# Chunked attention and a cosine feed-forward layer: turning the probabilities of tiles 2 to 8 with tall VectorE transposes and DMAs between partitions

## The chip, the core and the metric

The kernel runs on one core of a Trainium2 chip. The core has five engines, each with its own instruction queue that runs in program order: TensorE (PE; its weight loads are shown as PEld), VectorE (DVE), ScalarE (ACT), GpSimd (POOL) and SyncE (SP, which here issues all DMAs). The metric is the device time of one execution in microseconds (us); a kernel's time is the median of several runs. Matmuls read SBUF and write PSUM; everything is float32, and a matmul of full precision is made of three products of high and low parts.

## The reference

Attention inside chunks of 64 positions, then a feed-forward layer with g = h cos(h):

```python
# q, k, v: (8 batches, 8 heads, 576 positions, 64), chunks of 64
scores = scale * matmul(q_c, k_c.T)               # 64 x 64 for each batch, head and chunk
attn = exp(scores - max(scores)); attn = attn / (sum(attn) + 1e-9)
out = matmul(attn, v_c)
x = out.transpose(0, 2, 1, 3).reshape(4608, 512)  # 4608 tokens, 8 heads x 64
h = x @ w_in                                      # 512 -> 2048
g = h * cos(h)
result = g @ w_out                                # 2048 -> 512
```

## The kernel before

The 4608 tokens are nine tiles of 512 (t = 0 to 8). A tile has eight chunks, and the eight heads are four pairs (hp = 0 to 3, two heads h each); g is a pair of pairs (hps 2g and 2g+1).

**Attention of a tile.** `scores` makes the 64x64 products of queries and keys in two PSUM banks, VectorE and ScalarE make the probabilities e from them (maximum, difference, exponential, sum, `quotient`). A tile e of 128 partitions holds for each pair two rows of chunks: partition is (parity of the half, query), the free axis (chunk or head, key). For the product with the values the probabilities must be turned: the key goes on the partition. `weighted` (L757) then multiplies each turned 64x64 block (moving operand) with the values (stationary operand), 32 float32 matmuls that show up as 64 matmul instructions, and ScalarE takes the result out into e (L781 or L1609).

**How the probabilities are turned** differs by tile:
- tiles 0 and 1: `transposed` (L725), TensorE transposes of 128x128 against an identity (L731); these stay as they are.
- tile 2: `turned` (L740), for each pair eight VectorE instructions that transpose the 32x32 blocks of 32 partitions x 256 elements and put them where they belong.
- tiles 5 and 7: `turned_together` (L1576), the same for two pairs at once: eight instructions of 32 partitions x 512 for each g.
- tiles 3, 4, 6 and 8: `turned_by_pe` (L1582), four TensorE transposes for each pair (L1585) into a PSUM bank, and a copy by ScalarE or VectorE into the tile pts. Here the scores are laid out by head (`by_head`), the products are made by `weighted_turned` (L1589), and the values must come in another order: `load_values_turned` (L1508) loads them in four DMAs of 64 KB for each pair, in pieces of 512 bytes. The other tiles load them with one DMA of 256 KB (`load_v`).

**The feed-forward layer.** Tiles 0 and 1 are computed plainly (`hidden`, `activated`, `project`); tile 2 and then the pairs of tiles (3, 4), (5, 6) and (7, 8) by a Strassen-like scheme of seven products, for which VectorE, ScalarE and GpSimd make sums and differences and split them in high and low parts (`forms` for x, `split` in `outer` for g). The weights' sums lie in DRAM and are streamed in blocks of 512 KB through six rooms (`load_block`); a block is asked for when the matmuls of the block six before it are done.

**The order of the work.** No engine decides at run time: the program emits one order for each engine. For the first part (tiles 0 and 1, attention of tile 2) it comes from `placed` and `in_order`, with the priorities in the list DUE; for the rest from `planned` (L299) with offsets in MOVED. Both go through estimated durations and lags. In `planned` the main matmuls form one chain; the small matmuls of attention (`main=False`) are put on TensorE at the first seam at which their inputs are estimated to be there, plus CARE = 0.8 us. All DMAs stand in one queue on SP: one that waits for a semaphore holds all that stand behind it.

**Rooms.** `attention_of` (L1981) takes a pair of tiles (ta, tb): it begins both, loads values, and ends both (`attention_ends`, L1613). For tiles 3 and 4 (`alone`) pts has its own two buffers; for tiles 5 to 8 the two pairs of a g share one room of w_in.

Of the kernel before, what the change touches and what calls it, by code (L numbers as in the profile page):

```python
# [11 lines left out]
F32 = mybir.dt.float32  # L12
# [9 lines left out]
P = 128  # L22
TOK = 512
# [78 lines left out]

AHEAD = 4.0
# [27 lines left out]
    158.12, 58.9, 68.58, 63.65, 252.88, 143.8, 82.3, -250.55, 219.35, 114.51, -120.22, -295.86, 1e+09, -4.71,  # L131
# [5 lines left out]
    262.3, 48.25, 126.32, 193.62, 1e+09, 345.43, 23.97, -61.67, 75.14, -1.8, 433.58, 246.37, -62.79, 87.68, -8.61,  # L137
    -145.35, 32, 6.23, 84.32, 191.91, -66.13, 267.53, -107.91, 1e+09, 59.88, 1e+09, 1.78, 1e+09, 6.61, 1e+09,
    1e+09, -10.09, -254.05, 202.29, -15.1, 262.24, -166.36, 249.63, 71.08, 209.64, -226.64, 255.17, -18.33,
# [5 lines left out]
    -76.27, 1e+09, 292.24, -11.78, -101.18, 119.54, 173.07, 246.81, -59.42, 152.58, 59.6, 147.63, -111.18,  # L145
    -165.31, 170.18, 412.05, -234.16, 253.81, 56.94, 223.55, 174.74, 172.68, 262.87, 1e+09, -113.14, 133.26,
# [8 lines left out]
    199.71, 243.39, -154.74, 16.19, 1e+09, 1e+09, 143.88, -50.34, 1e+09, 1e+09, 1e+09, 1e+09, 1e+09, 1e+09,  # L155
    172.37, 92.61, 1e+09, 1e+09, 1e+09, 1e+09, 1e+09, 1e+09, 1e+09, 58.67, 248.55, 155.33, -25.97, 231.79, 141.91,
    1e+09, 1e+09, 153.74, 117.79, 119.81, 83.59, 470.08, 488.44, 258.14, 542.25, -17.83, 164.19, 314.55, 83.71,
    62.74, 350.71, -36.4, 242.13, -61.82, 228.28, 332.92, 1e+09, 437.5, 104.97, 27.99, 78.88, 1e+09, 458.39,
    -62.42, 304.54, 227.74, 1e+09, 424.55, 137.98, 50.14, 154.55, 190.64, 238.98, 240.92, 295.04, 313.65, -63.39,
    266.72, 327.78, 178.57, 212.45, 346.38, 151.22, 291.83, -2.81, 148.05, 154.34,  # L160
# [276 lines left out]
def attention_then_cos_ffn(ctx: ExitStack, tc, qT, kT, v, w_in, w_out, out, wide):  # L437
# [207 lines left out]
    def scores(t, g, banks, by_head=False, by_chunk=False):  # L645
# [3 lines left out]
        for j in range(2):  # L649
            qt, kt = queries.pop((t, 2 * g + j))  # L650
            for c in range(NCH):
# [10 lines left out]
        order_of = "(h r)" if by_head else "(r h)"  # L662
        e = weights_of(t, g).rearrange(f"p a {order_of} k -> p a r h k", h=2)
# [60 lines left out]
    def transposed(t, hp):  # L724
# [1734 lines left out]
```

## Time and profile before

| | |
|---|---|
| median of 3 runs | 806.09 us (805.15 to 806.11) |
| span of the profiled execution, first to last instruction | 804.7 us |
| TensorE busy, matmuls | 791.9 us (98%) |
| TensorE busy, weight loads | 700.4 us (87%) |
| VectorE busy | 692.5 us (86%) |
| ScalarE busy | 530.4 us (66%) |
| GpSimd busy | 203.7 us (25%) |
| DMA | 189.88 MB, 236 GB/s on average |

Busy times are averages over stages with different limits; matmuls are pipelined, and their ends are modelled. Which engine sets the time is read from the stretches and from the chain of work that ended last: it goes back from the last instruction, at each step to what released it.

### The profile page before, as it was taken

The numbers are of one execution on the slowest core, as the hardware profiler recorded it, in microseconds if no ns is written. First come the engines' busy times: TensorE is split into PE (matmuls) and PEld (weight loads), VectorE is DVE, ScalarE is ACT, GpSimd is POOL, SyncE is SP. The second block draws the span as 40 slices with busy tenths as digits, with TensorE's granted clock in tenths as the row PEclk, the third lists the DMA queues.
The fourth block names the chain that finished last, engine by engine and source line by source line (L and its number), as shares of the span: only waits on it lengthen the run. The fifth ranks groups of instructions, "written<-read, shape, count | busy, mean of one in ns | idle before, by whom it ended". The sixth has DMA issues, their size and how long they took to land.

```text
span 804.7 us, 17487 instructions
## 1 busy us (share of the span) xinstructions
PE 791.9 (98%) x6720; PEld 700.4 (87%) x6720; DVE 692.5 (86%) x1071; ACT 530.4 (66%) x1006; POOL 203.7 (25%) x179
## 2 busy tenths in 40 slices
PE   5999999999999999999999999999999999999998
PEld 5888788888988888888999998888999988889998
DVE  6899998888888798999999988899999878789854
ACT  4998856455567756767777566889655566665552
POOL 2373765866812211410410001121001001000000
PEclk9999999999999999999999999999999999999999
DMA  9993748585898896987557779655665665556653
GB/s 319 405 416 117 244 150 295 202 292 198 280 315 249 297 296 222 293 286 260 189 169 257 221 238 323 205 195 192 225 213 195 190 222 191 183 183 210 210 184 105
DMA packets 95266, 189.88 MB, mean 236 GB/s; under 512 B 8656, under 2 KB 51664, under 8 KB 95184
## 3 DMA queue, kind: packets, MB, share of 16 engines
q1 hardware_dynamic: 95184, 188.78, 69.0%
q8 instruction: 53, 0.87, 0.4%
q14 instruction: 29, 0.24, 0.1%
HBM read 148.90 MB, written 39.85 MB: 235 GB/s over the span
## 4 chain that ended last, share of the span: by engine, by line
PE 89%; DMA 4%; DVE 4%; ACT 2%; issue 1%; SPq 0%; DVEq 0%
PE acc L471 55%; PE h L471 29%; PE a L471 5%; DMA w_in<-in_w_in_dram 2%; DMA kt<-in_kT_dram 1%; DVE w L536 1%; PE a L1585 1%; DMA qt<-in_qT_dram 1%; DVE g L832 0%; ACT w L541 0%; ACT g L833 0%; DVE w_in L481 0%; ACT half L543 0%; DVE w_out L475 0%; DVE w_out L481 0%
## 5 line engine op out<-in xcount | busy, mean ns | idle before, releaser
L471 PE MATMUL h<-x,w_in 128*128 128x512 f32 (+1 forms) x852 | 190.6, 367 | 0.0
L471 PEld LDWEIGHTS h<-x,w_in 128*128 128x128 f32 x852 | 148.0, 188 | 27.7 <-DVE g L834 0.3
L471 PE MATMUL acc<-w_in,w_in 128*128 128x512 f32 (+1 forms) x702 | 153.0, 346 | 0.0
L471 PEld LDWEIGHTS acc<-w_in,w_in 128*128 128x128 f32 x702 | 113.5, 188 | 16.5
L471 PE MATMUL acc<-w_out,g_hi 128*128 128x512 f32 x352 | 110.0, 394 | 0.4 <-DVE vt L475 0.4
L471 PE MATMUL acc<-w_in,g_hi 128*128 128x256 f32 x576 | 104.2, 282 | 0.0
L471 PEld LDWEIGHTS acc<-w_in,g_hi 128*128 128x128 f32 x576 | 88.4, 188 | 0.9
L471 PE MATMUL acc<-x,w_in 128*128 128x512 f32 x276 | 82.6, 391 | 0.0
L471 PE MATMUL acc<-w_in,g_lo 128*128 128x256 f32 x288 | 80.3, 279 | 0.0
L471 PEld LDWEIGHTS acc<-w_out,g_hi 128*128 128x128 f32 x352 | 64.2, 188 | 13.3 <-DVE vt L475 0.8
L471 PE MATMUL acc<-w_out,g_lo 128*128 128x512 f32 x176 | 68.7, 391 | 0.0
L1483 ACT ACTIVATE w_out<-w_out 128x512 f32<-128x512 f32 x96 | 60.1, 631 | 11.5 <-DVE w_out L1479 11.2
L481 DVE TENSOR_TENSOR g_lo<-w_out,g_hi 128x512 fp32r<-128x512 f32 x79 | 57.2, 729 | 10.8 <-ACT g_hi L477 9.1
L477 ACT CAST g_hi<-w_out 128x512 fp32r<-128x512 f32 x75 | 46.4, 620 | 28.2 <-PE acc L471 15.6
L471 PEld LDWEIGHTS acc<-x,w_in 128*128 128x128 f32 x276 | 51.5, 188 | 11.1
L471 PEld LDWEIGHTS acc<-w_in,g_lo 128*128 128x128 f32 x288 | 54.3, 189 | 0.0
L481 POOL TENSOR_TENSOR w_out<-g,w_out 128x512 f32<-128x512 f32 x10 | 14.2, 1423 | 143.1 <-ACT w_out L1483 143.1
L477 ACT CAST g_hi<-g 128x512 fp32r<-128x512 f32 x50 | 30.8, 623 | 25.1 <-DVE g L834 12.4
L481 POOL TENSOR_TENSOR g_lo<-w_out,g_hi 128x512 fp32r<-128x512 f32 x8 | 11.7, 1466 | 127.7 <-ACT g_hi L477 53.9
L471 PE MATMUL h<-w_in,g_hi 128*128 128x256 f32 x240 | 43.5, 282 | 0.0
L471 PEld LDWEIGHTS acc<-w_out,g_lo 128*128 128x128 f32 x176 | 33.0, 188 | 7.1
L1476 ACT ACTIVATE w_out<-g 128x512 int32<-128x512 f32 x48 | 29.9, 630 | 13.6 <-DVE g L1492 12.2
(216 smaller groups left out, 1690.9 us busy)
## 6 DMA issues: line engine op xcount, KB each, us to landing
w_in<-combo SPq DMA_DIRECT2D x112, 512.0 KB, 4.3
w_in<-sums SPq DMA_DIRECT2D x84, 512.0 KB, 3.8
combo<-w_in SPq DMA_DIRECT2D x56, 256.0 KB, 3.9
sums<-w_out SPq DMA_DIRECT2D x56, 256.0 KB, 4.4
qt<-in_qT_dram SPq DMA_DIRECT2D x36, 256.0 KB, 5.2
kt<-in_kT_dram SPq DMA_DIRECT2D x36, 256.0 KB, 5.4
w_in<-in_w_in_dram SPq DMA_DIRECT2D x16, 512.0 KB, 9.1
w_out<-in_w_out_dram SPq DMA_DIRECT2D x16, 512.0 KB, 9.9
```

The lines of the kernel that those rows point to most:

```text
L471: kept(nc.tensor.matmul(*args, **kw))
L477: kept(nc.scalar.copy(out=out, in_=in_))
L481: kept(eng.tensor_tensor(out, a, b, op=op))
L536: kept(nc.vector.scalar_tensor_tensor(bits, bits, 3, low, op0=ALU.logical_shift_left, op1=ALU.bitwise_or))
L1476: kept(nc.scalar.activation(n.bitcast(I32), h, AF.Identity, bias=0.25, scale=0.5 / math.pi))
L1483: kept(nc.scalar.activation(g, g, AF.Sin, bias=0.5 * math.pi))
L1585: kept(nc.tensor.transpose(out=pt[:, i * P : (i + 1) * P], in_=e[:, 2 * i : 2 * i + 2].rearrange("p c k -> p (c k)"), identity=ident,))
```

## The change

All tiles from 2 to 8 get the same way of turning, and the code of the others goes. For each unit (one pair of heads in tiles 2, 3 and 4; two pairs in tiles 5 to 8) there are now four steps:
1. one VectorE instruction over all 128 partitions (512 or 1024 elements each) transposes all 32x32 blocks in place of their partitions and sorts them in two areas of pts, by the half of the keys;
2. ScalarE (or VectorE) copies the second area to a spare part of e, which is dead by then;
3. `over`: two DMAs move 32 partitions each of the first area to the second area of 32 other partitions (pieces of 1 KB, or 2 KB for two pairs);
4. `back`: two DMAs move what stood in the second area, from the spare copy, to the first area.

Half of the blocks thereby change partitions, the other half stand right from the start. The turned block of a chunk and head is now two runs of 32 columns, and `weighted` takes it so. The TensorE transposes at L1585, their copies out of PSUM, `by_head`, `weighted_turned` and `load_values_turned` are gone; the values of all these tiles come in one DMA for each pair. The lists DUE and MOVED have new numbers throughout.

```diff
+CROSS = 3.0
...
-    def turned(t, hp):
-
-        pts = att.tile([P, TOK], F32, name="pts")
-        probs[t, hp] = pts
...
-        def piece(par, qb, kb):
-            i, o = (par * CH + x * BL for x in (qb, kb))
-            kept(nc.vector.transpose(out=dst[o : o + BL, :, qb], in_=src[i : i + BL, :, kb]))
...
+    def turned(t, hps, pts):
+
+        g, first = divmod(hps[0], 2)
+        n = len(hps)
+        e = weights_of(t, g)[:, first : first + n]
+        areas = pts.rearrange("p (x n) -> p x n", x=2)
+        spare = e.rearrange("p a c k -> p (a c k)")[:, : n * TOK // 2]
+        for j, hp in enumerate(hps):
+            probs[t, hp] = pts.rearrange("p (x a c q) -> p a c x q", x=2, a=n, q=BL)[:, j]
+
+        def turn_blocks():
+            kept(nc.vector.transpose(
+                out=pts.rearrange("p (x m q) -> p m x q", x=2, q=BL),
+                in_=e.rearrange("p a c (x k) -> p (a c) x k", k=BL),
+            ))
+
+        def put_by(by):
+            copy_by(by, spare, areas[:, 1])
+
+        def crossed(par, x):
+            i = par * CH + x * BL
+            return slice(i, i + BL)
+
+        def over():
+            for par in range(2):
+                load(areas[crossed(par, 0), 1], areas[crossed(par, 1), 0])
+
+        def back():
+            for par in range(2):
+                load(areas[crossed(par, 1), 0], spare[crossed(par, 0)])
+
+        return turn_blocks, put_by, over, back
...
+                        q = pts[ks, fs] if t < FAST else pts[ks, 2 * pr + h]
                         matmul(
-                            banks[par][hs, o : o + CH], vt[ks, fs], pts[ks, fs],
+                            banks[par][hs, o : o + CH], vt[ks, fs], q,
...
                 def go(key=key, hp=hp):
-                    made[key] = turned(t, hp)
+                    made[key] = turned(t, (hp,), att.tile([P, TOK], F32, name="pts"))
                     made[key][0]()
-                pts.append(piece(DVE, 0.44, go, q[hp], w, *partial_out))
-                for i in range(1, 8):
-                    pts.append(piece(DVE, 0.44, rest_of(key, i), pts[-1]))
+                a = piece(DVE, 0.72, go, q[hp], w, *partial_out)
+                a = piece(ACT, 0.36, rest_of(key, 1), a, other=(DVE, 0.3, True))
+                a = piece(SP, 0.15, rest_of(key, 2), a, lag=CROSS)
+                pts.append(piece(SP, 0.15, rest_of(key, 3), a, lag=CROSS))
...
-    def load_values_turned(t, hp):
...
-        for s in range(2):
-            for c in range(2):
-                load(to[s * CH : (s + 1) * CH, :, c], src[c * CH : (c + 1) * CH, :, s])
-        values[t, hp] = vt
...
-            run = (lambda hp=hp: load_values_turned(t, hp)) if by_pe else (lambda hp=hp: load_v(t, hp))
-            v_rooms[t, hp].load = task(SP, 0.4 if by_pe else 0.1, run, new=(v_rooms[t, hp],), lag=5.0)
+            v_rooms[t, hp].load = task(SP, 0.1, lambda hp=hp: load_v(t, hp), new=(v_rooms[t, hp],), lag=5.0)
...
-    def turned_by_pe(t, hp, pt):
...
-        for i in range(NPR):
-            kept(nc.tensor.transpose(
-                out=pt[:, i * P : (i + 1) * P], in_=e[:, 2 * i : 2 * i + 2].rearrange("p c k -> p (c k)"), identity=ident,
...
-    def weighted_turned(t, g, banks):
...
-    def attention_ends(t, quotients, by_pe, alone=False):
+    def attention_ends(t, quotients, alone=False):
...
-            if by_pe:
...
-                for par in range(2):
-                    for qb in range(2):
-                        for kb in range(2):
...
-                                turned_together(t, g, pair_of_pts[t, g], qb, kb, par)
-                            done.append(task(
-                                DVE, 0.75, go, *(done[-1:] or [quotients[hp] for hp in hps]), uses=(e,) if first else (e, *pts_rooms),
...
+            for some in ((hps[:1], hps[1:]) if alone else (hps,)):
+                r = room_of("pts", 2) if alone else room_of(f"w_in{G_ROOM}")
+                rooms.append(r)
+                key = ("t", t, some)
+
+                def begin(some=some, key=key):
+                    if alone:
+                        pts = att.tile([P, TOK], F32, name="pts")
+                    else:
+                        pts = w_in_room(G_ROOM, F32)[:, PAD : PAD + 2 * TOK]
+                    made[key] = turned(t, some, pts)
+                    made[key][0]()
+
+                n = len(some)
+                a = task(DVE, (0.68, 1.2)[n - 1], begin, *(quotients[hp] for hp in some), new=(r,), uses=(e,))
+                a = task(ACT, (0.34, 0.58)[n - 1], rest_of(key, 1), a, uses=(r, e), other=(DVE, (0.3, 0.4)[n - 1], True))
+                a = task(SP, 0.15, rest_of(key, 2), a, uses=(r,), lag=CROSS)
+                done.append(task(SP, 0.15, rest_of(key, 3), a, uses=(r, e), lag=CROSS))
...
-            run = weighted_turned if by_pe else lambda t, g, b: weighted(t, (2 * g, 2 * g + 1), b)
             w = task(
-                PE, 1.1, made_by(key, lambda g=g, run=run: run(t, g, (bank("a", 0), bank("a", 1)))), *done,
-                *(v_rooms[t, hp].load for hp in hps), new=banks, uses=(*pts_rooms, *(v_rooms[t, hp] for hp in hps)),
+                PE, 1.1, made_by(key, lambda g=g: weighted(t, (2 * g, 2 * g + 1), (bank("a", 0), bank("a", 1)))), *done,
+                *(v_rooms[t, hp].load for hp in hps), new=banks, uses=(*rooms, *(v_rooms[t, hp] for hp in hps)),
...
```

## Rows read from the trace of the kernel before

**Rows 1.** Part 1 of the page: busy us, share of the span, instructions.
```profile
PE 791.9 (98%) x6720; PEld 700.4 (87%) x6720; DVE 692.5 (86%) x1071; ACT 530.4 (66%) x1006; POOL 203.7 (25%) x179
```

**Rows 2.** Stretches of 20 us: busy time of each engine, granted clock, DMA share, GB/s.
```profile
0.00:20.00 20.00, 11.41 (x264) 10.28 (x264) 12.15 (x24) 8.90 (x16) 4.42 (x10) 0.97 0.92 320
20.00:40.00 20.00, 19.80 (x205) 16.71 (x202) 17.76 (x31) 18.13 (x35) 6.60 (x5) 0.94 1.01 403
40.00:60.00 20.00, 20.00 (x156) 16.53 (x155) 19.73 (x27) 18.37 (x34) 14.51 (x11) 1.00 1.03 416
...
780.00:800.00 20.00, 20.00 (x172) 20.00 (x171) 10.01 (x15) 6.89 (x12) 0.00 (x0) 1.00 0.37 126
```

**Rows 3.** The chain in order of time: start us, us, what.
```profile
86.03 2.36 PE acc L471 x9
...
302.38 2.72 PE acc L471 x12
...
744.46 22.64 PE acc L471 x192
```

**Rows 4.** Waits of TensorE, longest first: us in total, times, longest us.
```profile
PE acc L471 <- DMA kt<-in_kT_dram: 4.9, 2, 4.4
PE a L471 <- DMA kt<-in_kT_dram: 3.2, 2, 1.7
PE acc L471 <- DVE vt L475: 0.4, 1, 0.4
```

**Rows 5.** Line L1585: durations in ns min/median/max, first and last start in us.
```profile
L1585 PE MATMUL a<-ident,w_in x48: 270/272/273, 268.6 to 631.5; 128*128 128x128 f32 x48
...
L1585 PE MATMUL a<-ident,e x16: 270/272/273, 248.5 to 260.2; 128*128 128x128 f32 x16
```

**Rows 6.** The chain from 620 to 630 us.
```profile
620.32 1.09 PE a L471 x64
...
623.74 0.44 PE a L1585 x4
624.17 0.71 PE acc L471 x6
```

**Rows 7.** Part 4 of the page: the chain by line.
```profile
PE acc L471 55%; PE h L471 29%; PE a L471 5%; DMA w_in<-in_w_in_dram 2%; DMA kt<-in_kT_dram 1%; DVE w L536 1%; PE a L1585 1%; DMA qt<-in_qT_dram 1%; DVE g L832 0%; ACT w L541 0%; ACT g L833 0%; DVE w_in L481 0%; ACT half L543 0%; DVE w_out L475 0%; DVE w_out L481 0%
```

**Rows 8.** Groups of VectorE instructions: form, count | busy us, mean ns | idle before.
```profile
L1580 DVE STREAM_TRANSPOSE w_in<-e 32x512 f32<-32x512 f32 x32 | 22.5, 702 | 0.7
L834 DVE TENSOR_TENSOR g<-h,g 128x512 f32<-128x512 f32 x31 | 21.1, 681 | 0.6
...
L748 DVE STREAM_TRANSPOSE pts<-e 32x256 f32<-32x256 f32 x32 | 13.8, 434 | 1.2 <-PE a L471 0.6
```

**Rows 9.** Groups of ScalarE instructions, the same columns.
```profile
L477 ACT COPY h<-h 128x256 f32<-128x256 f32 x16 | 5.7, 359 | 9.1 <-PE h L471 9.0
...
L477 ACT COPY w_in<-a 128x512 f32<-128x512 f32 x9 | 5.1, 588 | 4.9 <-PE a L471 2.6 <-PE a L1585 2.4
```

**Rows 10.** SP: issues in order of time, issue durations in ns, waits.
```profile
606.98 5.96 SPq L468 DMA_DIRECT2D vt<-in_v_dram  x8
...
L468 SPq DMA_DIRECT2D kt<-in_kT_dram x36: 328/428/1499, 1.2 to 494.5; - x36
...
SPq L468 <- PE acc L471: 246.7, 108, 5.2
```

**Rows 11.** DMA issues by tile: count, KB each, median us from issue to landing.
```profile
w_in<-combo SPq DMA_DIRECT2D x112, 512.0 KB, 4.3
...
vt<-in_v_dram SPq DMA_DIRECT2D x32, 64.0 KB, 3.3
qt<-in_v_dram SPq DMA_DIRECT2D x32, 64.0 KB, 3.9
...
partial<-pts SPq DMA_DIRECT2D x2, 256.0 KB, 2.0
...
out_dram<-kt SPq DMA_DIRECT2D x2, 128.0 KB, 1.7
```

More of the change, by code (lines that the diff above doesn't have):

```diff
@@ L643, in scores_early, with scores @@
         return [largest, below, lowered, raised_and_summed]
-    def scores(t, g, banks, by_head=False, by_chunk=False):
+    def scores(t, g, banks, by_chunk=False):
         for j in range(2):
@@ L661, in scores @@
                     )
-        order_of = "(h r)" if by_head else "(r h)"
-        e = weights_of(t, g).rearrange(f"p a {order_of} k -> p a r h k", h=2)
+        e = weights_of(t, g).rearrange("p a (r h) k -> p a r h k", h=2)
         found = []
@@ L681, in raised @@
                 for r in range(NPR):
-                    c = h * NPR + r if by_head else 2 * r + h
+                    c = 2 * r + h
                     kept(nc.scalar.activation(
@@ L737, in transposed @@
         return lambda by: copy_by(by, pts, pt)
-    def turned(t, hp):
-        pts = att.tile([P, TOK], F32, name="pts")
-        probs[t, hp] = pts
-        src = weights_of(t, hp // 2)[:, hp % 2].rearrange("p c (x k) -> p c x k", k=BL)
-        dst = pts.rearrange("p (c x q) -> p c x q", x=CH // BL, q=BL)
-        def piece(par, qb, kb):
-            i, o = (par * CH + x * BL for x in (qb, kb))
-            kept(nc.vector.transpose(out=dst[o : o + BL, :, qb], in_=src[i : i + BL, :, kb]))
-        nb = CH // BL
-        return [
-            lambda x=(par, qb, kb): piece(*x)
-            for par in range(2) for qb in range(nb) for kb in range(nb)
-        ]
+    def turned(t, hps, pts):
[23 more added lines that the diff above has]
+        return turn_blocks, put_by, over, back
     def weighted(t, hps, banks):
@@ L1498, in attention_then_cos_ffn @@
     x_ready = {}
-    pair_of_pts = {}
     def load_queries(t, after=()):
@@ L1506, in load_queries, with load_values_of, attention_begins @@
         return made_q
-    def load_values_turned(t, hp):
-        name, bufs = ("vt", 2) if hp < 2 else ("qt", HP)
-        vt = att.tile([P, TOK], F32, name=name, bufs=bufs)
-        to = vt.rearrange("p (r c x) -> p r c x", r=2, c=2)
-        src = v[t, hp].rearrange("p (r s x) -> p r s x", r=2, s=2)
-        for s in range(2):
-            for c in range(2):
-                load(to[s * CH : (s + 1) * CH, :, c], src[c * CH : (c + 1) * CH, :, s])
-        values[t, hp] = vt
-    def load_values_of(t, by_pe):
+    def load_values_of(t):
         for hp in range(HP):
             v_rooms[t, hp] = room_of("vt", 2) if hp < 2 else room_of("qt", HP)
-            run = (lambda hp=hp: load_values_turned(t, hp)) if by_pe else (lambda hp=hp: load_v(t, hp))
-            v_rooms[t, hp].load = task(SP, 0.4 if by_pe else 0.1, run, new=(v_rooms[t, hp],), lag=5.0)
-    def attention_begins(t, queries_in, by_pe):
+            v_rooms[t, hp].load = task(SP, 0.1, lambda hp=hp: load_v(t, hp), new=(v_rooms[t, hp],), lag=5.0)
+    def attention_begins(t, queries_in):
         by_chunk = t in BY_PARTS
@@ L1536, in attention_begins @@
             s = task(
-                PE, 1.1, made_by(key, lambda g=g: scores(t, g, (bank("a", 0), bank("a", 1)), by_pe, by_chunk)),
+                PE, 1.1, made_by(key, lambda g=g: scores(t, g, (bank("a", 0), bank("a", 1)), by_chunk)),
                 *(q[0] for q in qs), new=(e, *banks, *m), uses=[r for q in qs for r in q[1:]], at=12.0 if t == 3 else 0.0,
@@ L1571, in attention_begins @@
         ]
-    def pts_pair():
-        return w_in_room(G_ROOM, F32)[:, PAD : PAD + 2 * TOK].rearrange("p (a n) -> p a n", a=2)
-    def turned_together(t, g, pts, qb, kb, par):
-        src = weights_of(t, g).rearrange("p a c (x k) -> p (a c) x k", k=BL)
-        dst = pts.rearrange("p a (c x q) -> p (a c) x q", x=CH // BL, q=BL)
-        i, o = (par * CH + x * BL for x in (qb, kb))
-        kept(nc.vector.transpose(out=dst[o : o + BL, :, qb], in_=src[i : i + BL, :, kb]))
-    def turned_by_pe(t, hp, pt):
-        e = weights_of(t, hp // 2)[:, hp % 2]
-        for i in range(NPR):
-            kept(nc.tensor.transpose(
-                out=pt[:, i * P : (i + 1) * P], in_=e[:, 2 * i : 2 * i + 2].rearrange("p c k -> p (c k)"), identity=ident,
-            ))
-    def weighted_turned(t, g, banks):
-        for j, hp in enumerate((2 * g, 2 * g + 1)):
-            pts = probs.pop((t, hp)).rearrange("p (h r c q) -> p h r c q", h=2, r=2, c=2)
-            vt = values.pop((t, hp)).rearrange("p (r c h d) -> p r c h d", r=2, c=2, h=2)
-            for r in range(2):
-                for c in range(2):
-                    for s in range(2):
-                        ks = slice(s * CH, (s + 1) * CH)
-                        o = (4 * j + 2 * r + c) * CH
-                        for h in range(2):
-                            hs = slice(h * CH, (h + 1) * CH)
-                            matmul(
-                                banks[s][hs, o : o + CH], vt[ks, r, c, h], pts[ks, h, r, c],
-                                start=(o == 0), stop=True, skip_group_check=True,
-                            )
-        x = weights_of(t, g).rearrange("p a (r s c) q -> p a r s (c q)", r=2, s=2)
-        def taken_out(s):
-            xq = banks[s].rearrange("p (a r n) -> p a r n", a=2, r=2)
-            kept(nc.scalar.copy(out=x[:, :, :, s], in_=xq))
-        return [lambda: taken_out(0), lambda: taken_out(1)]
-    def attention_ends(t, quotients, by_pe, alone=False):
+    def attention_ends(t, quotients, alone=False):
         for g in range(2):
@@ L1617, in attention_ends @@
             hps = (2 * g, 2 * g + 1)
+            rooms = []
             done = []
-            if alone:
-                pts_rooms = [room_of("pts", 2), room_of("pts", 2)]
-            else:
-                pts_rooms = [room_of(f"w_in{G_ROOM}")]
-            if by_pe:
-                for hp in hps:
-                    b = room_of(f"a{hp % 2}")
-                    key = ("t", t, hp)
-                    def turn_it(hp=hp, key=key):
-                        made[key] = bank("a", hp)
-                        turned_by_pe(t, hp, made[key])
-                    i = task(PE, 0.4, turn_it, quotients[hp], new=(b,), uses=(e,))
-                    def taken(by, hp=hp, key=key):
-                        if alone:
-                            pts = att.tile([P, TOK], F32, name="pts")
-                        else:
-                            if hp % 2 == 0:
-                                pair_of_pts[t, g] = pts_pair()
-                            pts = pair_of_pts[t, g][:, hp % 2]
-                        probs[t, hp] = pts
-                        copy_by(by, pts, made[key])
-                    r = pts_rooms[hp % 2] if alone else pts_rooms[0]
-                    fresh = alone or hp % 2 == 0
-                    done.append(task(
-                        ACT, ACT_TOK, taken, i, *done, new=(r,) if fresh else (), uses=(b,) if fresh else (b, r),
-                        other=(DVE, DVE_TOK),
-                    ))
-            else:
-                first = True
-                for par in range(2):
-                    for qb in range(2):
-                        for kb in range(2):
-                            def go(par=par, qb=qb, kb=kb, first=first, g=g, hps=hps):
-                                if first:
-                                    pair_of_pts[t, g] = pts_pair()
-                                    for hp in hps:
-                                        probs[t, hp] = pair_of_pts[t, g][:, hp % 2]
-                                turned_together(t, g, pair_of_pts[t, g], qb, kb, par)
-                            done.append(task(
-                                DVE, 0.75, go, *(done[-1:] or [quotients[hp] for hp in hps]), uses=(e,) if first else (e, *pts_rooms),
-                                new=pts_rooms if first else (),
-                            ))
-                            first = False
-                done = done[-1:]
@@ L1984, in attention_of @@
             queries_in[ta] = load_queries(ta)
-        qa = attention_begins(ta, queries_in[ta], alone)
-        load_values = lambda t, by_pe: load_values_of(t, by_pe)
+        qa = attention_begins(ta, queries_in[ta])
         queries_in[tb] = load_queries(tb)
-        qb = attention_begins(tb, queries_in[tb], True)
-        load_values(ta, alone)
-        attention_ends(ta, qa, alone, alone)
-        load_values(tb, True)
-        attention_ends(tb, qb, True, alone)
+        qb = attention_begins(tb, queries_in[tb])
+        load_values_of(ta)
+        attention_ends(ta, qa, alone)
+        load_values_of(tb)
+        attention_ends(tb, qb, alone)
     attention_of(0, True)
```

12 lines of the change are left out of this document (removed), and 118 rows, old and new, of tables (DUE, MOVED).

## The prediction

> **What bounds the kernel now.** Busy shares come first: TensorE 98%, VectorE 86%, ScalarE 66% [rows 1]. They alone don't settle it, since matmuls overlap and a busy TensorE need not be a full one. The 20 us stretches come next: from 40 us on TensorE is busy for all 20.00 us of nearly every stretch, at full granted clock, while VectorE moves between 10 and 20 [rows 2]; only the first two stretches have holes (11.41 and 19.80). The chain that ended last decides. Up to 86 us it runs through loads, VectorE and ScalarE; from 86.03 us to the end it holds TensorE and nothing else, and in the last stage 192 matmuls of 128x256 take 22.64 us, 0.118 us each without a hole [rows 3]. TensorE's own waits say the same: the longest are loads of keys at the start, the rest is 0.4 us and less [rows 4]. So after 86 us each microsecond of instructions that leaves TensorE leaves the time, if nothing new makes TensorE wait; VectorE work saved there is worth nothing by itself.
>
> A rule against this reading: the Trainium skill (Perfetto Trace Analysis, Identifying the Most-Contended Engine) says that matmul busy time is a poor measure and that weight-load busy time is a better one. By it TensorE would have 13% of headroom (weight loads 87%, [rows 1]), and removing instructions could come to nothing. The trace disagrees: the spacing of the matmuls in the chain is constant [rows 3]. The sum would be 0 by the rule and 7.1 us by the chain.
>
> **The change, part by part.** *TensorE transposes of tiles 3, 4, 6 and 8 go.* They are 48 + 16 = 64 instructions at L1585 [rows 5], sixteen groups of four. In the chain a group of four takes 0.44 us, and the neighbouring matmuls keep their pace (6 in 0.71 us) [rows 6]; the chain's share of that line, 0.9% of 804.7 us, is 7.2 us [rows 7]. I take 16 x 0.445 = 7.1 us. All of it lies on the path, since all of it is later than 86 us. As many matmuls with the probabilities remain: a group of 64 costs 1.09 us [rows 6] and there are 14 such groups in tiles 2 to 8. Their moving operand is now two runs of 32 columns where it was one run of 64. No row has that form on TensorE; the bounds are 0 and a doubling, 14 x 1.09 = 15.3 us. I take 0: VectorE writes runs of 32 at L748 and L1580 at about 1.05 ns per column, the same pace at which it does plain work [rows 8], so SBUF gives short runs freely there.
>
> *VectorE.* Out go 32 pieces of 0.434 and 32 of 0.702 us, 36.3 us together [rows 8]. In come 12 instructions of 128x512 and 8 of 128x1024. From the two forms, (702 - 434)/256 = 1.05 ns per column; 512 columns cost 0.70 and 1024 cost 1.24 us if the height is free: 12 x 0.70 + 8 x 1.24 = 18.3 us. The height isn't shown for this operation. If four heights cost four times as much, it is 73 us; if less than now, nothing is gained. I take the lower end, because a plain 128x512 instruction takes 0.681 us [rows 8], as much as the transpose of a quarter of the height. So VectorE falls by 18 us, off the path: 0 us.
>
> *ScalarE* loses 16 copies out of PSUM of 0.588 us (9.4 us) and gains 12 copies of half the size (0.359) and 8 of about 0.59: 9.0 us [rows 9]. Some of either kind may be VectorE's. No change: 0 us, covered by ScalarE's idle third.
>
> *Loads.* The values of tiles 3, 4, 6 and 8 come in 16 loads of 256 KB, no longer in 64 pieces of 64 KB. Eight of those took SP 5.96 us to issue, 0.745 each [rows 10]: 47.7 us less, 16 x 0.43 = 6.9 us more. The 80 new DMAs of 32 or 64 KB (20 units: two across, two back) have no price in the trace of before; by 0.33 us, the shortest issue of a load of keys [rows 10], to 0.745 each they cost 26 to 60 us of SP. I take 0.43, the median of those loads, as the new ones have a quarter of the pieces of the 64 KB loads (34 us): SP comes out 7 us better, with 19 us worse as the bound. The bytes are few: 48 x 32 KB and 32 x 64 KB, 3.6 MB.
>
> *The new waits.* After VectorE's transpose and the copy, SP issues the DMAs across (waiting for the copy), then those back (waiting until the ones across have landed, since they overwrite what those read), and the 64 small matmuls wait for these. So between copy and matmuls there are two landings, one after the other, where there was none. The plan allows 3.0 us of landing and 0.15 of issue for each, and for tiles 3 to 8 another 0.8 us ahead of small matmuls: 7.1 us, plus about half a main step (0.35 to 0.7 us), since TensorE takes the matmuls up at the next seam. TensorE runs in program order, so whatever is later than that stalls it. What is a landing? The nearest rows: 64 KB loads in 3.3 and 3.9 us (median, with up to 0.4 us more of issue than the new ones need and other traffic ahead of them), stores of 256 KB in 2.0, of 128 KB in 1.7 with an empty queue [rows 11]. Two hops, with 0.35 us for the second DMA of each: 4.1 us at the low end, 8.5 at the high one. I take 3.3 for the way across and 2.0 for the way back, since SP has sent nothing between the two and the queue has drained: 5.3 + 0.7 = 6.0 us, under 7.1. Stall: 0.
>
> The Trainium skill (DMA: Bandwidth & Descriptors, Anatomy of one DMA) gives a fixed 2.0 us per DMA plus bytes by 436 GB/s: an estimate of 2.15 us for 64 KB, 4.3 for two in a row. With 0.7 us of issue, by it the stall is 0 with 2.1 us to spare; the measured 3.3 to 3.9 are longer, and they decide.
>
> Behind the waiting SP stand the 512 KB block loads, the next tile's queries, keys and values, and the stores. SP waits now too: 246.7 us for matmuls to free rooms [rows 10]. A block serves 12 matmuls of 128x512 or 24 of 128x256, 2.7 to 2.8 us; with six rooms it is asked for five blocks ahead, 13.6 us, and lands in 4.3 [rows 11]: 9.3 us of cover against a hold of two to four. If it were gone, each microsecond beyond would stall the main matmuls one for one.
>
> *The order.* Both lists of priorities, for all stages, are replaced; so the first 86 us, bound by loads, VectorE and ScalarE, are rearranged as well though none of their operations is removed. TensorE's holes there are 8.6 + 0.2 us in the first 40 [rows 2], most of them ahead of the first keys. I take 0, with 3 us either way.
>
> Sum: -7.1 in the profiled execution, 804.7 to 797.6; the median of the runs is 1.4 us above that span, so 806.1 - 7.1 = 799.0 us.
>
> **The rivals.**
> 1. *Part of the gain is given back at the small matmuls.* If the way across takes 3.9 us and the way back 3.3, the two are 7.2 + 0.7 = 7.9 us, against 7.1 and the half step: 0.1 to 0.45 us late, by 14 groups 1.4 to 6.3 us: 800.4 to 805.3. For it: loads for the next tile are issued in the same stretches. Against it: SP, while held, sends nothing that could be ahead.
> 2. *Slower, by the same waits.* From 7.1/14 = 0.51 us late per group the gain is gone: with 7.6 us for allowance and seam that is two landings of 3.7 us on average. At 4.3 us each (queries, keys and blocks ahead, as where the 64 KB pieces took 3.9), the two are 9.3 us, 1.7 late, 14 x 1.7 = 24 us: 823. Place: TensorE before the matmuls at L772. Against it: the low rows, and that TensorE has no wait for any DMA after the start [rows 4] with allowances for loads that are near their median too.
> 3. *The tall transpose takes four times as long* (2.8 and 5.0 us): 55 us more on VectorE than I count, 2.1 to 3.8 us later per unit than planned, with 14 groups 30 us and more: 830. Against it: the plain 128x512 instruction.
> 4. *The change does not take TensorE's time*, because the two-run operand costs what the transposes gave (0.51 of 1.09 us per group) or a new front order loses it: 806.
>
> **How the numbers follow.** Forecast (799.0, with 3 us either way from the first 86 us): 0.62. Rival 1: 0.20, all but a tail of it faster. Rival 2: 0.08. Rival 3: 0.03. Rival 4: 0.07, mostly no change. A measurement of this kernel tells 0.2%, 1.6 us, from no change. Faster 0.81, same 0.07, slower 0.12. The range for 8 in 10 takes in the forecast with its order bound and nearly all of rival 1: 796 to 805.
>
> **What would show it.** No instruction of TensorE on an identity after 86 us, and a chain that is still TensorE to the end: right. Twenty tall transposes of 0.70 and 1.24 us: the VectorE term. TensorE waits that name a DMA into the tile of turned probabilities: rival 1 below 0.5 us per group, rival 2 above it. Groups of 64 small matmuls longer than 1.09 us: rival 4. VectorE's busy time near 675 us says that the saving is there and unused. The forecast is wrong if TensorE's waits after 86 us sum to more than 2 us, or if the chain leaves VectorE and ScalarE later than at 88 us.

## The result and the profile after

The changed kernel takes 813.51 us in the median (810.48 to 816.78) against 805.62 for the kernel before: a ratio of 1.0101, 95% interval 1.0072 to 1.0130. It is 1% slower, where 799.0 us was forecast and 805 was the upper end of the range. The profiled execution took 814.66 us, with a span of 812.8 (804.7 before): 8.1 us more.

Part 1 of the page of the changed kernel, to be read against [rows 1]:

```profile
PE 790.2 (97%) x6656; PEld 697.3 (86%) x6656; DVE 677.8 (83%) x1015; ACT 534.0 (66%) x1015; POOL 221.1 (27%) x188
```

All that was to leave has left: 64 matmuls fewer, VectorE 14.7 us less. Yet the span grew, so TensorE must stand still somewhere. Its waits, longest first (us in total, times, longest us), stand against [rows 4]:

```profile
PE acc L489 <- DMA kt<-in_kT_dram: 4.4, 2, 4.2
PE a L489 <- DMA kt<-in_kT_dram: 3.8, 2, 2.4
PE a L489 <- DMA pts<-w_in: 2.8, 2, 1.5
PE a L489 <- DMA pts<-e: 2.6, 2, 2.3
PE a L489 <- issue: 2.5, 3, 1.7
PE a L489 <- DMA w_in<-e: 0.6, 1, 0.6
```

The first two are the loads of keys at the start, as before. The others are new. The small matmuls (a) wait for DMAs into pts and into the room of w_in that holds the turned probabilities: the transfers that the change adds. (The 1.7 us under "issue" are such a wait too: they are the wait in the chain below, which ends at 608.11 us, and the second of the two DMAs that the matmuls there need lands at 608.20.)

Where they stand in time, in stretches of the span (columns as in [rows 2]); a stretch without a wait shows full busy time there:

```profile
0.00:40.00 40.00, 30.52 (x459) 26.38 (x460) 29.23 (x52) 26.14 (x48) 10.41 (x15) 0.96 0.97 364
160.00:200.00 40.00, 37.53 (x280) 30.29 (x279) 27.69 (x41) 21.09 (x43) 16.50 (x16) 1.00 0.68 232
240.00:280.00 40.00, 39.48 (x410) 34.72 (x409) 33.94 (x63) 27.74 (x56) 20.00 (x16) 1.00 0.76 239
280.00:320.00 40.00, 36.69 (x307) 31.59 (x306) 32.20 (x46) 22.13 (x44) 8.93 (x8) 0.96 0.69 236
440.00:480.00 40.00, 39.07 (x489) 38.32 (x488) 30.82 (x43) 23.21 (x39) 4.45 (x3) 1.00 0.78 244
600.00:640.00 40.00, 38.04 (x427) 37.55 (x426) 29.53 (x42) 20.43 (x34) 2.60 (x2) 1.00 0.61 197
```

In the five later stretches TensorE is idle for 2.47 + 0.52 + 3.31 + 0.93 + 1.96 = 9.2 us. In the same stretches the kernel before was idle for 0.04 us in all; its least full one:

```profile
240.00:280.00 40.00, 39.96 (x485) 35.24 (x484) 33.06 (x63) 29.48 (x56) 11.80 (x10) 1.00 0.87 278
```

Two thirds of the 9.2 us lie in tiles 2 to 4 (up to 320 us). From 280 to 320 us the granted clock is 0.96 as well: 0.04 of 36.7 us, 1.5 us more. In the first 40 us TensorE was busy for 0.7 us less than in [rows 2] (30.52; 11.41 + 19.80 before). That is 11.4 us of a loss of 8.1 + 7.1 = 15.2. The 0.7 us can be chance: e1_no_dma below is the same kernel up to the first new DMA, at 145 us, and was busy for 32.05 us there. Of the other 3.8 a part is in the small groups themselves, since one that waited takes longer (1.33 us in the chain below, where 1.09 is usual); the rest is in no row here (ends of matmuls are modelled, so a wait can hide in a busy time).

One group of the pair (5, 6), read along the chain (start us, us, what):

```profile
606.46 1.66 issue
608.11 1.33 PE a L489 x64
```

and SP's queue just before, in order of time:

```profile
599.11 1.15 SPq L486 DMA_DIRECT2D w_in<-w_in  x2
601.52 0.33 SPq L486 DMA_DIRECT2D w_in<-sums  x1
601.94 0.40 SPq L486 DMA_DIRECT2D out_dram<-kt  x1
603.57 1.15 SPq L486 DMA_DIRECT2D w_in<-e  x2
```

The two DMAs across are issued at 599.11, those back at 603.57, and the matmuls begin at 608.11: 9.0 us, where 6.0 were forecast and 7.1 allowed. Between the two SP has sent a block of 512 KB and a store of 256 KB, and the way back stands behind both: it lands 4.5 us after its issue. Landings of all of them (count, KB, median us), against [rows 11]:

```profile
w_in<-w_in SPq DMA_DIRECT2D x24, 64.0 KB, 3.6
pts<-pts SPq DMA_DIRECT2D x24, 32.0 KB, 3.1
pts<-e SPq DMA_DIRECT2D x16, 32.0 KB, 1.8
w_in<-e SPq DMA_DIRECT2D x8, 64.0 KB, 2.0
pts<-w_in SPq DMA_DIRECT2D x8, 32.0 KB, 3.1
```

### The profile page after: what moved, and what is told of

It is laid out like the page before. It is cut to its first block, busy times and chain, and to the rows that moved or that the text cites. A ratio compares the mean times of both kernels' runs of the same rounds, so it can differ in the third digit from the quotient of the medians.

```text
span 812.8 us, 17418 instructions
## 1 busy us (share of the span) xinstructions
PE 790.2 (97%) x6656; PEld 697.3 (86%) x6656; DVE 677.8 (83%) x1015; ACT 534.0 (66%) x1015; POOL 221.1 (27%) x188
## 4 chain that ended last, share of the span: by engine, by line
PE 84%; DMA 6%; DVE 4%; ACT 3%; issue 2%; SPq 1%; POOL 0%; ACTq 0%; POOLq 0%
PE acc L489 52%; PE h L489 27%; PE a L489 5%; DMA pts<-pts 2%; DMA kt<-in_kT_dram 1%; DMA w_in<-w_in 1%; DMA qt<-in_qT_dram 1%; SPq L486 1%; ACT w L559 1%; ACT half L561 0%; DVE w L554 0%; DMA pts<-e 0%; DMA pts<-w_in 0%; DVE g L866 0%; DVE z L729 0%
## 5 line engine op out<-in xcount | busy, mean ns | idle before, releaser
L499 DVE TENSOR_TENSOR g_lo<-w_out,g_hi 128x512 fp32r<-128x512 f32 x76 | 52.0, 689 | 22.5 <-ACT g_hi L495 20.6
L495 ACT CAST g_hi<-w_out 128x512 fp32r<-128x512 f32 x81 | 50.1, 622 | 28.7 <-PE acc L489 15.8
L499 POOL TENSOR_TENSOR g_lo<-w_out,g_hi 128x512 fp32r<-128x512 f32 x11 | 15.7, 1430 | 155.7 <-ACT g_hi L495 100.0
L499 DVE TENSOR_TENSOR g_lo<-g,g_hi 128x512 fp32r<-128x512 f32 x44 | 41.1, 937 | 5.4 <-ACT g_hi L495 4.2
L499 POOL TENSOR_TENSOR w_out<-g,w_out 128x512 f32<-128x512 f32 x13 | 17.5, 1356 | 92.2 <-ACT w_out L1519 88.4
```

The lines of the kernel that those rows point to most:

```text
L495: kept(nc.scalar.copy(out=out, in_=in_))
L499: kept(eng.tensor_tensor(out, a, b, op=op))
```

## The experiments

Theory A: the change does what it should for TensorE, and the two landings in a row are later than allowed because of what SP sends around them. Rivals: the two-run operand or the new order costs the time; the allowance is only too small; SP's queue itself is slow; the DMAs are long whatever one does.

| kernel | median us (lowest to highest) | ratio to before, 95% interval |
|---|---|---|
| changed kernel | 813.51 (810.48 to 816.78) | 1.0101 (1.0072 to 1.0130) |
| e1_no_dma | 799.32 (798.71 to 800.61) | 0.9923 (0.9903 to 0.9943) |
| e2_cross45 | 841.32 (839.54 to 847.89) | 1.0457 (1.0409 to 1.0505) |
| e3_one_hop | 808.31 (807.13 to 811.57) | 1.0035 (1.0020 to 1.0050) |
| e4_pool | 827.83 (827.19 to 832.36) | 1.0287 (1.0253 to 1.0320) |
| e5_together | 802.84 (800.03 to 805.36) | 0.9963 (0.9951 to 0.9974) |
| e6_plan_two | 808.45 (805.44 to 809.60) | 1.0025 (1.0012 to 1.0039) |
| e7_plan_one | 806.15 (803.16 to 809.31) | 1.0008 (0.9992 to 1.0023) |
| e8_hold | 824.41 (820.79 to 824.58) | 1.0202 (1.0170 to 1.0233) |

Kernels were run with the kernel before beside them (805.95, 806.10 and 806.14 us), so the ratios are what compares; 0.1% is 0.8 us.

**e1_no_dma**: the 80 new DMAs are left out, and nothing else; half of the blocks then stay in the wrong place.

```diff
             for par in range(2):
-                load(areas[crossed(par, 0), 1], areas[crossed(par, 1), 0])
+                pass
...
-                load(areas[crossed(par, 1), 0], spare[crossed(par, 0)])
+                pass
```

> The changed kernel with the 80 DMAs between partitions left out (the crossed blocks then stay in the wrong place, so the result is not attention's; every other instruction and the order of each engine stay). Theory A (the matmuls of the weighted values wait for two landings in a row): of the 15.3 us that TensorE lost more than before, about 10.5 us at eight of the fourteen groups and 2 us in a stretch at the lower clock behind the longest stall go, and the 7 us of the transposes come to light: 799 to 802 us, no wait of TensorE on the turned probabilities. Rival B (the new order of all other work costs the time, and the DMAs only lie there): 808 us or more.

Measured: 799.32 us, with a span of 797.3; the forecast's own sum for the span was 797.6. TensorE's waits are loads of keys at the start, the longest 4.2 us, and sums of GpSimd, the longest of these:

```profile
PE h L748 <- POOL e L499: 1.6, 2, 1.3
```

No wait for turned probabilities is left. The two-run operand, the tall transposes, the copies and the new order are all in this kernel, so none of them costs the gain. The DMAs alone cost 1.0101 - 0.9923 = 1.78%, 14.3 us.

**e2_cross45**: only the planner's allowance for a landing is raised.

```diff
-CROSS = 3.0
+CROSS = 4.5
```

> The changed kernel with the plan's allowance for a landing raised from 3.0 to 4.5 us, nothing else. Theory A: the plan now allows 9.0 us for two landings and 0.8 more; measured from the first issue across to the last landing back they took 4.1 to 9.1 us, so at most one or two groups are late: 799 to 804 us. Rival B: a new order is as good or bad as the other, 808 to 816 us. Third theory C (attention has no room for 3 us more in each unit and the sums for the next pair of tiles come late): 805 to 815 us with TensorE waiting at the first main matmuls of the pairs of tiles 5, 6 and 7, 8, not at the small groups.

Measured: 841.32 us, a miss. The longest waits are no longer those of the small matmuls:

```profile
PE h L489 <- ACT pts L495: 5.0, 1, 5.0
PE h L489 <- DVE g L499: 3.9, 2, 3.3
```

The main matmuls (h) wait for ScalarE and VectorE. The offsets in MOVED are numbers of the plan that they were made for, and with another allowance the whole order is another one. The run says that the allowance can't be changed alone; it says nothing on how long a landing is.

**e3_one_hop**: the copy takes both areas, and all four DMAs read the copy. The way back no longer waits for the way across to land, only for the copy; the order of all queues is the same.

```diff
-        spare = e.rearrange("p a c k -> p (a c k)")[:, : n * TOK // 2]
+        spare = e.rearrange("p a c k -> p (a c k)")
+        kept_areas = spare.rearrange("p (x n) -> p x n", x=2)
...
-            copy_by(by, spare, areas[:, 1])
+            copy_by(by, spare, pts)
...
-                load(areas[crossed(par, 0), 1], areas[crossed(par, 1), 0])
+                load(areas[crossed(par, 0), 1], kept_areas[crossed(par, 1), 0])
...
-                load(areas[crossed(par, 1), 0], spare[crossed(par, 0)])
+                load(areas[crossed(par, 1), 0], kept_areas[crossed(par, 0), 1])
```

> The changed kernel, order of every engine unchanged, but the copy takes both areas (128x512 or 128x1024 in place of half of it, 0.25 to 0.45 us longer), and all four DMAs of a unit read the copy, so those back no longer wait for those across: one landing in place of two. Theory A: from copy to matmuls 2.2 us of issue and one landing of 2 to 4.4 us, 4.2 to 6.6 us against 7.1 us allowed: 799 to 803 us. Rival B: 810 to 816 us.

Measured: 808.31 us, 0.66% (5.3 us) less than the changed kernel. It lies between the two theories: the second landing in the row is a good third of the loss (less what the longer copy costs), not all of it. What is left stands in SP's queue:

```profile
593.41 1.15 SPq L486 DMA_DIRECT2D w_in<-e  x2
595.82 0.33 SPq L486 DMA_DIRECT2D w_in<-sums  x1
596.24 0.40 SPq L486 DMA_DIRECT2D out_dram<-kt  x1
596.68 1.15 SPq L486 DMA_DIRECT2D w_in<-e  x2
```

The second pair could go at 594.6, but a block stands ahead of it whose room comes free at 595.82 only; it goes at 596.68.

**e4_pool**: the changed kernel with the 80 DMAs issued by GpSimd, in a queue of their own.

```diff
+    def cross(out, in_):
+        kept(nc.gpsimd.dma_start(out=out, in_=in_))
...
-                load(areas[crossed(par, 0), 1], areas[crossed(par, 1), 0])
+                cross(areas[crossed(par, 0), 1], areas[crossed(par, 1), 0])
...
-                load(areas[crossed(par, 1), 0], spare[crossed(par, 0)])
+                cross(areas[crossed(par, 1), 0], spare[crossed(par, 0)])
```

> The changed kernel with the 80 DMAs between partitions issued by GpSimd, on a queue of its own, no longer by SP; places in the order unchanged. Theory A1 (a landing is long because the block loads issued on SP's queue between across and back, 512 KB each, drain first): landings near 2 us, stalls at the groups gone, 799 to 804 us unless GpSimd's own work, which now stands behind the waiting DMAs, comes late. Theory A2 (the 16 DMA engines are shared, whatever the queue): landings of 3 to 4.5 us behind loads as before, 810 us or more.

Measured: 827.83 us, and the landings are no shorter than in SP's queue:

```profile
w_in<-w_in POOLq DMA_DIRECT2D x24, 64.0 KB, 3.6
pts<-e POOLq DMA_DIRECT2D x16, 32.0 KB, 3.9
w_in<-e POOLq DMA_DIRECT2D x8, 64.0 KB, 3.8
```

The ways back, 1.8 and 2.0 us from SP, take 3.9 and 3.8 here. A queue of one's own therefore doesn't pass the bytes that others have under way, which fits 16 DMA engines that all queues share. That DMAs issued by GpSimd are slow in themselves is not the reason: the shortest of these landings took 1.7 us, as from SP. (GpSimd's DMAs stand in program order behind its own work too, and TensorE waits up to 5.6 us for them, so the time of this kernel is not the price of the landings alone.)

**e5_together**: e3_one_hop, and the four DMAs are issued at the place of those across.

```diff
                 load(areas[crossed(par, 0), 1], kept_areas[crossed(par, 1), 0])
+                load(areas[crossed(par, 1), 0], kept_areas[crossed(par, 0), 1])
...
             for par in range(2):
-                load(areas[crossed(par, 1), 0], kept_areas[crossed(par, 0), 1])
+                pass
```

> As the kernel with one landing (all four DMAs of a unit read a copy of both areas, order of every engine unchanged), but the two DMAs back are issued right behind the two across, no longer at their own later place on SP, where a block load that waits for TensorE to free its room and that then sends 512 KB stood ahead of them. In the one-landing kernel the last landing came 4.7 to 8.9 us behind the first issue in the units of tiles 5 to 8, of which the way to their own place took about 3 us. Theory A (what counts is how much later than planned the last DMA lands): 2.2 us of issue and 2 to 4 us of landing, stalls of 5 to 6 us in all go: 800 to 804 us. Rival D (SP is what is short: 80 issues of 0.5 to 0.6 us and the loads behind them): no gain over 808.3, or a loss, with TensorE waiting for blocks or values.

Measured: 802.84 us, 0.72% (5.8 us) less than e3_one_hop, and 0.37% less than the kernel before: it is faster than both. The same unit in SP's queue, and the waits that name turned probabilities (the longest; one more of 0.4 us):

```profile
591.42 2.42 SPq L486 DMA_DIRECT2D w_in<-e  x4
...
PE a L489 <- DMA pts<-w_in: 2.1, 1, 2.1
```

Nothing waits in tiles 5 to 8 any more (every stretch of 40 us from 320 to 760 is full). Of the 0.40% (3.2 us) that still divide it from e1_no_dma, 2.5 us are these waits, in tiles 2 to 4.

**e6_plan_two** and **e7_plan_one**: two landings as in the change, or one with all four DMAs issued together as in e5_together, with a plan for tiles 3 to 8 made anew: new offsets in MOVED, the measured issue times for SP, and 4.5 us for a landing with its issue (e7: 2.2 us of issue for four DMAs and one landing of 3.4).

```diff
+LANDS = 3.4
...
-                a = task(SP, 0.15, rest_of(key, 2), a, uses=(r,), lag=CROSS)
-                done.append(task(SP, 0.15, rest_of(key, 3), a, uses=(r, e), lag=CROSS))
+                a = task(SP, 1.1, rest_of(key, 2), a, uses=(r,), lag=LANDS)
+                done.append(task(SP, 1.1, rest_of(key, 3), a, uses=(r, e), lag=LANDS))
```

> The changed kernel with two landings in a row as it is, but in the plan of tiles 3 to 8 each pair of DMAs takes 1.1 us of SP and 3.4 us to land (4.5 in place of 3.15), the other loads and stores 0.33 to 1.5 us of SP as measured, and the offsets MOVED are replaced by new ones that were searched for this plan; tile 2 keeps its plan. By the plan TensorE idles 3.5 us. Theory A: the groups of tiles 3 to 8 wait no longer, tile 2 still waits 2.5 us; 799.3 + 3.5 + 2.5, so 803 to 808 us; the 841 us with the larger allowance alone came from offsets that belonged to another plan. Theory C (attention has no room for later small matmuls): 815 us and more, with waits of TensorE at main matmuls.

> One landing, all four DMAs of a unit issued together, and the plan told so for tiles 3 to 8: a copy of 0.6 or 1.05 us, 2.2 us of SP, 3.4 us to land, the other DMAs' SP time as measured, offsets searched anew. By the plan TensorE idles 3.3 us. Theory A: 799.3 + 3.3, so 800 to 805 us, no wait for turned probabilities. Theory C: 810 us and more.

Measured: 808.45 and 806.15 us. In e6_plan_two the waits for turned tiles are gone but for one of 2.0 us in tile 2, whose plan was not touched, and a few tenths. e6_plan_two lies just above its range of 803 to 808 us.

So allowing the measured landing does remove the waits. But the main matmuls now wait elsewhere, for VectorE's and ScalarE's results (1.3 us and less each in e6_plan_two): TensorE is idle there for 1.2, 1.1 and 1.6 us in the three stretches of 40 us from 200 to 320. I can't tell how much of that is the room the longer allowance takes and how much a worse order, since the offsets are not those of the change. Neither came near the 802.84 us of e5_together, and e7_plan_one missed its expectation (800 to 805 us and no wait for turned probabilities; two of them, 1.0 us together, are left).

**e8_hold**: the changed kernel with its two landings, but the DMAs back right behind those across in SP's queue.

```diff
                 load(areas[crossed(par, 0), 1], areas[crossed(par, 1), 0])
+            for par in range(2):
+                load(areas[crossed(par, 1), 0], spare[crossed(par, 0)])
...
             for par in range(2):
-                load(areas[crossed(par, 1), 0], spare[crossed(par, 0)])
+                pass
```

> The change as it is, with its two landings one after the other, but the two DMAs back are issued at the place of those across, right behind them: SyncE is held until the way across has landed, and sends nothing between the two. This is the situation that the prediction assumed. Theory A (the prediction's size of the two landings was wrong because SyncE sends block loads and stores between across and back, and the DMAs back come late by that): across to back takes the 5.6 us of the quiet unit at 541 us in the changed kernel, within the 7.1 us allowed; the waits of TensorE for turned tiles fall to under 3 us together, and the time to 800 to 805 us. Theory B (a landing is long whatever stands between, since the block loads are outstanding already when the DMAs across are issued): the two take 7 to 8 us again, the waits stay, 808 to 814 us. Theory C (holding the queue costs as much): the waits for turned tiles shrink, but main matmuls, VectorE or ScalarE wait for blocks and loads held back for 2 to 4 us in 20 places; over 808 us with waits that name w_in<-sums, w_in<-combo, kt or qt after 100 us.

Measured: 824.41 us: none of the three as a whole, but the clearest answer of all. It sets up the very situation that the prediction had assumed, a held queue that sends nothing between. Landings of the ways back, then TensorE's waits:

```profile
pts<-e SPq DMA_DIRECT2D x16, 32.0 KB, 1.8
w_in<-e SPq DMA_DIRECT2D x8, 64.0 KB, 2.0
pts<-w_in SPq DMA_DIRECT2D x8, 32.0 KB, 1.8
...
PE a L489 <- DMA pts<-w_in: 6.8, 2, 4.7
PE a L489 <- DMA pts<-e: 5.8, 5, 3.2
```

These tiles' names tell ways back alone (those of w_in<-w_in are mixed with ways across). Their medians are 1.8 to 2.0 us, the 2.0 of the prediction; pts<-w_in took 3.1 in the changed kernel. And the groups of tiles 5 to 8 don't wait at all (no w_in<-w_in, no w_in<-e; all stretches from 320 to 800 us are full). There theory A holds: from the first issue across to the last landing back a unit of these tiles takes 4.8 to 7.6 us, in the changed kernel 4.5 to 9.1 (the quiet unit that the expectation names stands at 544 us there). But in tiles 2 to 4 TensorE waits 12.6 us for turned tiles, and its holes cost clock as well:

```profile
160.00:200.00 40.00, 36.48 (x266) 29.60 (x265) 27.07 (x41) 20.47 (x43) 15.31 (x16) 0.91 0.67 230
280.00:320.00 40.00, 32.90 (x301) 28.74 (x302) 22.71 (x37) 14.77 (x34) 5.86 (x5) 0.84 0.67 214
```

From 160 to 320 us it is idle for 14.0 us (0.4 in e1_no_dma), and by an estimate from these two rows the clock costs 0.09 of 36.5 and 0.16 of 32.9 us, 8.6 us more: 22 of the 22.5 us that the ratios put between this kernel and e1_no_dma. Two units of these tiles in SP's queue:

```profile
284.75 2.48 SPq L486 DMA_DIRECT2D pts<-pts  x2
291.48 1.14 SPq L486 DMA_DIRECT2D pts<-w_in  x2
...
293.34 1.14 SPq L486 DMA_DIRECT2D pts<-pts  x2
296.80 1.14 SPq L486 DMA_DIRECT2D pts<-w_in  x2
```

In these tiles a group of small matmuls needs two units. The first way across goes out behind loads of queries and keys and takes 6.7 us until the way back can go; the second unit isn't issued before that, at 293.34, and its way back at 296.80. Four landings in a row stand ahead of one group. No main matmul waits for a block, so the cover of the blocks held even here.

## Why the prediction was wrong

**Right, and shown.** Removing the TensorE transposes is worth about what the sum said: by the ratio, e1_no_dma is 0.77% (0.57 to 0.97) faster than the kernel before, 6.2 us of the 7.1 summed. That its span, 797.3 us, meets the 797.6 so closely is in part luck: in the first 40 us its profiled execution ran at a granted clock of 1.00, that of the kernel before at 0.97 and 0.94 [rows 2]. The doubt from the busy share of weight loads is settled by it too: they stood at 87% and the time fell all the same. The operand of two runs cost nothing here: a group of 64 still takes 1.09 us in the changed kernel where it doesn't wait (chain, 475 us):

```profile
475.43 1.09 PE a L489 x64
```

The tall transposes take 0.70 and 1.24 us; two of VectorE's four groups stand here (form, count | busy us, mean ns | idle before), and with the other two, 4.9 and 2.8 us, they sum to 18.2 us, where 18.3 was forecast; rival 3 falls:

```profile
L767 DVE STREAM_TRANSPOSE pts<-e 128x512 f32<-128x512 f32 x8 | 5.5, 702 | 0.2
L767 DVE STREAM_TRANSPOSE w_in<-w_in 128x1024 f32<-128x1024 f32 x4 | 5.0, 1244 | 2.6 <-PE a L489 2.6
```

The saved VectorE time was worth nothing, as forecast. ScalarE changed by 3.6 us, off the path. What the new order may cost in the first 40 us, 0.7 us or nothing, is within the bound of 3. No main matmul waits for a streamed block.

**The step that failed** is "The new waits": "I take 3.3 for the way across and 2.0 for the way back, since SP has sent nothing between the two and the queue has drained: 5.3 + 0.7 = 6.0 us, under 7.1. Stall: 0." Three things in it were wrong.

1. The way across was taken at the median of 64 KB loads [rows 11], 3.3. It stands behind whatever is under way (loads of values and blocks at these three places), and where a group waits it could be longer, as the chains of the changed kernel show at 167, 264 and 442 us:

```profile
167.69 6.00 DMA pts<-pts
264.28 6.20 DMA pts<-pts
442.82 5.10 DMA w_in<-w_in
```

The longest wait in one piece, 2.3 us at 175 us, belongs here, and to point 3: SP is held between across and back and sends nothing, as the prediction assumed, and the way back takes 1.8 us. SP's queue there, the DMAs of two units:

```profile
167.69 2.55 SPq L486 DMA_DIRECT2D pts<-pts  x4
173.71 2.82 SPq L486 DMA_DIRECT2D pts<-e  x4
```

2. SP does send in between. The DMAs across and back are two steps of the planned order, and the plan, which sees 3 us of landing between them, fills the gap with blocks and stores. At 599 us, shown above, the way back took 4.5 us behind them; another, late in the chain of the changed kernel:

```profile
627.79 4.67 DMA w_in<-w_in
```

Where nothing had been put in between, the 2.0 us held even in the changed kernel (units at 154, 167, 396 and 544 us: 1.8 to 2.0), and in e8_hold it held for nearly all (the longest took 2.5). Something in between doesn't always cost: behind the block sent at 445.23 us the way back at 447.98 took 2.0 us all the same.

3. The working was made for one unit per group. Tiles 2, 3 and 4 need two units for a group, from one queue. In the changed kernel they mostly go out together, so that SP needs 2.6 us for the four DMAs across and 2.8 for the four back, as at 167 us above; from the first issue to the last landing 10.1 us pass there. Two thirds of the idle time are in these tiles.

How the waits divide among the three isn't shown. What the prediction allowed was right: in tiles 5 to 8 of the changed kernel the four groups whose units took 4.5 to some 7.5 us don't wait, and the four with 8.1 to 9.1 us do, where 7.1 us and about half a main step were counted.

Besides, issuing one of these DMAs takes 0.51 to 0.58 us in the median, not 0.43: for 80 of them 10 us more of SP, so by the prediction's own sum SP comes out some 3 us worse and not 7 better (that sum, 47.7 - 6.9 - 34.4, is 6.4).

The outcome is that of rival 2, in its place (TensorE ahead of the small matmuls) and past its point of 0.51 us per group (9.2 us of idle time by 14 groups is 0.66, without the clock). Only its size was off: it forecast 24 us by making every group 1.7 us late; the waits are 0.3 to 2.8 us in eight of the 14 groups, and the loss is 14.3 us. (The waits that name a DMA into turned tiles sum to 6.3 us, 0.45 per group, which by itself would be rival 1's mark; those under "issue" and the idle time within groups carry it over.) Its chance of 0.08 was too low for a reason that the trace of before did show: SP waits for rooms and sends whatever comes next [rows 10], so "SP, while held, sends nothing" needed a look at the planned order between the two steps, not only at the queue's rule.

**How the 14.3 us divide**, by the ratios: making the two ways independent gives 5.3 us back (e3_one_hop), issuing them together another 5.8 (e5_together), and 3.2 remain, most of them the waits for the one landing in tiles 2 to 4.

## What to carry to other kernels

A DMA that is put between two engines can cost what is under way when it is issued (here 1.8 to 6.2 us for 32 or 64 KB), and an engine that waits for it holds all its own later work: count, for each consumer, all landings in a row, over all units it needs, and read the planned order for what is sent between them. Where two small transfers depend on each other only because one overwrites what the other reads, a larger copy on an engine with room makes them independent; then issue them together. An instruction removed from the bound engine gives its time only if what replaces it is early, so a gain of 0.5 us per group is easily lost to a transfer that is 1 us late.

## What the runs showed of the hardware

- The time from issue to landing of a 32 or 64 KB DMA between partitions was 1.8 to 2.0 us where the queue had been held and up to 6.0 and 6.2 us where loads of values and blocks were under way. The Trainium skill (DMA: Bandwidth & Descriptors, Anatomy of one DMA) gives a fixed 2.0 us and bytes by 436 GB/s, fitted to DMAs that GpSimd issues; by an estimate that is 2.1 us for these. The medians of e8_hold, from SP, agree with it; the others are up to three times as long, so here its sum is the low end.
- Issuing from GpSimd's queue did not shorten it: medians of 3.5 to 4.2 us, the shortest 1.7.
- A VectorE transpose of 32x32 blocks over 128 partitions took as long as over 32: 702 ns for 512 elements a row, before [rows 8] and after.
- A hole in TensorE's work can cost clock as well. In stretches of 2 us (columns as above) around the longest one:

```profile
286.00:288.00 2.00, 0.80 (x32) 0.70 (x32) 1.59 (x4) 0.42 (x1) 2.00 (x3) 1.00 0.84 262
288.00:290.00 2.00, 0.72 (x25) 0.71 (x28) 1.02 (x2) 0.00 (x0) 0.94 (x1) 0.83 0.69 213
290.00:292.00 2.00, 2.00 (x24) 1.59 (x18) 1.15 (x2) 1.55 (x3) 0.00 (x0) 0.50 0.97 382
```

The engine was busy for 0.80 and 0.72 of 2 us in two stretches running, and in the next the granted clock was 0.50, the level of 1.2 GHz, although it was fully busy again. The half clock of these 2 us is 1.0 us of the 1.5 above. The hole of 2.5 us at 174 us had no such effect (granted clock 1.00 from 160 to 200 us), and the one of 3.5 us at the same place in e8_hold had (0.91); what tells them apart stays open.
